# A fused attention and feed-forward kernel: the state of batch 0 is loaded by the ScalarE DMA queue instead of the SyncE queue

## Chip, cores and metric

The kernel runs on one core of one Trainium2 chip. The metric is the device time of one execution in microseconds (us), as the median of several runs.

## What is computed

For each of 8 batches and 8 heads there is a block `x` of 512 rows and a `state` of 32 rows, both 64 wide. Each attends to the other, and the joined rows (544 for each batch, 8 heads x 64 = 512 wide) go through a gated feed-forward layer with 1536 hidden columns. Inputs and output are float32.

```python
B, H, S, Ns, D = (8, 8, 512, 32, 64)
def _attn_ref(x, state):
    scores = scale * np.matmul(x, state.transpose(0, 1, 3, 2))
    a = softmax(scores)                      # over the 32 state rows
    xread = np.matmul(a, state)
    scores2 = scale * np.matmul(state, x.transpose(0, 1, 3, 2))
    a2 = softmax(scores2)                    # over the 512 rows of x
    sread = np.matmul(a2, x)
    return np.concatenate([xread, sread], axis=2)
def _moe_ref(x, w_gate, w_val, w_out):       # x: (8 * 544, 512)
    gate = np.maximum(x @ w_gate, 0.0)
    val = x @ w_val
    return gate * val @ w_out
```

(The softmax is written out in the reference; `scale` is 1/sqrt(64).)

## The kernel before

The attention output is never formed for the x rows. For each batch the kernel multiplies the state with the gate and value weights first (`u_mm`, L331, tile `u_ps`, evicted to `U`), and then the softmax weights, transposed (`ANS`), with `U` (`gv_mm`, L369, tile `gv_ps`). ScalarE takes the relu of the gate half (`gv_relu`, L381), VectorE multiplies it with the value half (`gv_mult`, L385), and `out_piece` (L407, tile `o_ps`) multiplies the result with the output weights. The rows of the state itself, 32 for each batch, come at the end for all batches together (`gvs`, L393).

The order of the instructions on each engine is written out by hand: the program is under a manual schedule (L462), so each engine runs its instructions in the order of the program text. First come L470 to L482: a memset for dummy matmuls, the identity matrix, a memset of `sz_b` on GpSimd (POOL), `st_dma(0, 1)` at L473 (the load of the state of batch 0), four loads of x of batch 0, two heads each (L474, L475, `x_dma` at L153), an activation on ScalarE (ACT) of a single column at L476, and VectorE (DVE) work for the permutation matrix (`make_perm`, L173) and columns of ones. Then the list `FIRST` (L17 to L65) is run through, a hand-made order of steps for batches 0 to 2; a loop over batches 2 to 7 (L527) does the rest. A step is a name and its arguments, with "a", "v" or "p" for ACT, DVE or POOL:

```python
FIRST = [
    ("dummy", 9), ("w", 0, 256, ("s", 0)), ("st_cast", 0, 1, "v"), ("st_mm", 0, 1), ("st", 1, 2),
    ("xl", 1, 0, 2, ("x", 0, 4)), ("xl", 1, 2, 2), ("xl", 1, 4, 2), ("xl", 1, 6, 2), ("st", 2, 3), ("dummy", 3),
    ("st_ev", 0, 1, "a"), ("conv", 0, 0, 2, "v"), ("xt", 0, 0), ("dummy", 1), ("conv", 0, 2, 2, "v"),
```

The names that matter here:

- `dummy` (L466): matmuls on zeros that keep TensorE (PE) busy.
- `st` (`st_dma`, L140): a load of state, 64 KB for one of the batches 0 to 2 (128 partitions of 512 bytes). `st_cast` (L181) turns it to bfloat16 (`st_b`), `st_mm` (L184) transposes it with four matmuls into `stT_ps`, and `st_ev` (L193) evicts that to `stT`.
- `xl` (`x_dma`): a load of x. A load of two heads has 256 KB, two runs of 1 KB in each partition. `conv` (L229) turns two heads to bfloat16 in `xs`, `xt` (L243) transposes them with four matmuls into `xT_ps`, `xe` (L248) evicts that to `xT`.
- `sc` (L254), `exp` (L270), `sum` (L275), `mul` (L280): scores, exponential on ACT, sum and reciprocal on DVE, product into `a_sn` on DVE or POOL. `at` and `ae` transpose `a_sn`.
- `w` (`w_dma`, L160): two loads of weights, gate and value, 256 columns each in the first steps (256 KB each), issued by POOL. `u` and `ue` are the matmuls of the state with these weights and their eviction, `g`, `gr`, `gm` the three steps of `gv`.

All loads of x and state, the DMA transposes and the stores are issued by the SyncE queue (SP), in the order of the program. `gate` (L135) makes a load wait for the landing of another: the first weight loads wait for the state of batch 0, `("s", 0)`; the loads of x of batch 1 wait for the third x load of batch 0, `("x", 0, 4)`; the second weight loads wait for the first gate weights.

Of the kernel before, what the change touches and what calls it, by code (L numbers as in the profile page):

```python
# [67 lines left out]
def kernel(  # L68
# [9 lines left out]
    nc = tc.nc  # L78
# [34 lines left out]
    st_f = const.tile([128, 3, 2, D], FP32, name="st_f")  # L113
# [21 lines left out]
    def gate(d, after):  # L135
        if after is not None:
            info = mybir.DependencyInfo(mybir.DependencyClass.Sync, mybir.DependencyReason.DATA)
            tc.add_manual_dep(d.ins, loads[after], info, reason="order of loads")

    def st_dma(lo, hi, after=None):  # L140
        if lo < 3:
            d = nc.sync.dma_start(out=st_f[:, lo:hi].rearrange("p b t d -> p b (t d)"),
                                  in_=state.rearrange("b h (m t) d -> (h m) b (t d)", t=2)[:, lo:hi])
        else:
            d = nc.sync.dma_start(out=sz_f.rearrange("p b g d -> p (b g) d"),
                                  in_=state[3:B].rearrange("b (g h) n d -> (h n) (b g) d", g=2))
        loads["s", lo] = d.ins.name
        gate(d, after)
# [322 lines left out]
    make_identity(nc, id128)  # L471
    nc.gpsimd.memset(sz_b, 0.0)
    st_dma(0, 1)  # L473
    for j in range(NJ):  # L474
        x_dma(0, 2 * j, 2)  # L475
# [5 lines left out]
    for i in range(3):  # L481
        set_ones(i)  # L482

    steps = {
        "dummy": dummies, "w": w_dma, "wo": wo_dma, "st": st_dma,
        "st_cast": st_cast, "st_mm": st_mm, "st_ev": st_ev, "st_z": st_z, "st_bar": st_bar, "conv": x_conv, "xc": x_copy, "xt": x_tr, "xe": x_ev,
        "sc": sc_mm, "exp": sc_exp, "sum": nrm_sum, "mul": nrm_mul, "at": a_tr, "ae": a_ev,
# [96 lines left out]
```

The softmax here doesn't subtract the row's maximum and nothing guards it: scores larger than these inputs give would overflow.

## Time and profile before

| | us |
|---|---|
| median of 8 runs | 225.65 |
| lowest and highest run | 224.53, 226.43 |
| the profiled execution, its time | 226.43 |
| the profiled execution, its span | 224.6 |
| busy in the span: PE, DVE, ACT, POOL | 216.7, 140.4, 114.3, 42.1 |
| `st_f` loads, issue to landing: shortest, longest | 1.8, 5.4 |
| `xf` loads of the first 6 us, issue to landing: shortest, longest | 2.9, 5.1 |

The span runs from the first instruction to the last. PE, DVE, ACT, POOL and SP are TensorE, VectorE, ScalarE, GpSimd and SyncE; PEld is TensorE's weight load; a q behind the name (SPq) is the engine's instruction queue, which issues DMAs. L156 is line 156 of the kernel; L128 and L126 are the helper `cp` on DVE and ACT. In a time line a row gives start and length in us, engine, line, operation, output<-input, shapes and the number of instructions, and in brackets how long the engine had been idle and what released it. The chain of waits goes back from the last instruction and names at each step what that step waited for.

### The profile page before, as it was taken

What the parts mean: (1) busy time and instruction counts of PE and PEld (TensorE: products, weight loads), DVE (VectorE), ACT (ScalarE), POOL (GpSimd) and SP (SyncE); (2) the same over time, 40 slices, a digit from 0 to 9 for tenths busy, and PEclk for the clock granted to TensorE, in tenths of its full rate; (3) what the DMA queues carried; (4) which work ended last, traced back from release to release, by engine and by line L of the source; (5) the groups of instructions that cost most, each with busy time, mean ns of one, the idle gap of its engine ahead of it and who ended that gap; (6) DMA issues with size and microseconds to landing.
All of it is one profiled execution on the core that took longest, in us unless ns stands there. A gap on an engine that the chain in (4) does not pass through costs nothing.

```text
span 224.6 us, 4848 instructions
## 1 busy us (share of the span) xinstructions
PE 216.7 (96%) x1931; PEld 107.2 (48%) x1953; DVE 140.4 (63%) x245; ACT 114.3 (51%) x212; POOL 42.1 (19%) x51
## 2 busy tenths in 40 slices
PE   7979999999999999999999999999999999999994
PEld 4654433344444444444444444444444444586543
DVE  5597889795577657866595659564956544442210
ACT  3656777576273647363745455455636344343112
POOL 6398004137070160007000700000000000000000
PEclk9997999999999999999999999999999999999999
DMA  5999998986954861295119811361131111110123
GB/s 179 247 223 188 218 247 156 214 204 157 234 160 103 234 139 50 56 271 129 53 39 268 143 47 47 96 146 50 47 93 57 47 47 50 47 47 28 69 74 113
DMA packets 43575, 28.17 MB, mean 125 GB/s; under 512 B 23840, under 2 KB 39328, under 8 KB 43552
## 3 DMA queue, kind: packets, MB, share of 16 engines
q1 hardware_dynamic: 36688, 23.14, 39.4%
q0 software_dynamic: 6864, 4.72, 14.3%
q8 instruction: 15, 0.25, 0.4%
q14 instruction: 8, 0.07, 0.1%
HBM read 18.35 MB, written 8.91 MB: 121 GB/s over the span
## 4 chain that ended last, share of the span: by engine, by line
PE 92%; DVE 2%; DMA 2%; issue 1%; SPq 1%; ACT 0%
PE o_ps L414 38%; PE gv_ps L377 38%; PE u_ps L325 6%; PE gvs_ps L399 5%; DMA xf<-in_x_dram 2%; PE sc_ps L260 2%; PE o_ps L439 1%; PE sr_ps L306 1%; DVE a_sn L283 1%; PE warm_ps L468 1%; SPq L156 1%; PE aT_ps L288 1%; DVE xs L128 0%; PE xT_ps L246 0%; DVE cs L277 0%
## 5 line engine op out<-in xcount | busy, mean ns | idle before, releaser
L386 DVE TENSOR_TENSOR h_sb<-gv_ps,g_sb 128x512 bf16<-128x512 f32 x96 | 65.7, 688 | 51.4 <-ACT g_sb L383 51.0
L377 PE MATMUL gv_ps<-ans,U 128*128 128x512 bf16 x384 | 95.3, 382 | 0.1
L414 PE MATMUL o_ps<-wo_sb,h_sb 128*128 128x512 bf16 x350 | 91.1, 379 | 1.4 <-issue 0.5
L383 ACT ACTIVATE g_sb<-gv_ps 128x512 bf16<-128x512 f32 x96 | 57.3, 597 | 54.7 <-PE gv_ps L377 53.9
L377 PEld LDWEIGHTS <-U 128*128 128x128 bf16 x384 | 36.2, 98 | 42.4 <-issue 1.8
L414 PEld LDWEIGHTS <-h_sb 128*128 128x128 bf16 x372 | 35.2, 98 | 43.4 <-issue 4.0
L126 ACT CAST U<-u_ps 128x512 bf16<-128x512 f32 x52 | 27.6, 595 | 7.1 <-PE u_ps L325 6.5
L128 DVE CAST U<-u_ps 128x512 bf16<-128x512 f32 x44 | 27.7, 674 | 1.7 <-PE u_ps L325 1.7
L130 POOL CAST xb<-xf 128x1024 bf16<-128x1024 f32 x11 | 11.2, 1041 | 72.0 <-DMA xf<-in_x_dram 72.0
L126 ACT COPY o_sb<-o_ps 128x512 f32<-128x512 f32 (+2 forms) x20 | 10.8, 540 | 18.7 <-PE o_ps L414 17.1
L128 DVE COPY o_sb<-o_ps 128x512 f32<-128x512 f32 (+2 forms) x18 | 11.4, 635 | 9.1 <-ACT o_sb L126 4.5
L271 ACT ACTIVATE e_sn<-sc_ps 128x512 bf16<-128x512 f32 (+1 forms) x18 | 9.8, 551 | 10.2 <-PE sc_ps L260 10.2
L403 DVE TENSOR_TENSOR hs_sb<-gvs_ps,g_sb 128x256 bf16<-128x256 f32 x12 | 5.1, 424 | 9.9 <-ACT g_sb L402 9.9
L130 POOL COPY xs<-xb 128x1024 bf16<-128x1024 bf16 x11 | 11.2, 1042 | 0.3
L277 DVE TENSOR_REDUCE cs<-e_sn 128x32 f32<-128x1024 bf16 (+2 forms) x13 | 10.4, 797 | 1.0 <-ACT e_sn L271 1.0
L325 PEld LDWEIGHTS <-stT 64*32 64x32 bf16 x560 | 6.0, 90 | 8.7 <-issue 7.0
L325 PE MATMUL u_ps<-wg_sb,stT 64*32 64x256 bf16 (+1 forms) x280 | 10.0, 318 | 0.0
L402 ACT ACTIVATE g_sb<-gvs_ps 128x256 bf16<-128x256 f32 x12 | 4.6, 384 | 10.2 <-PE gvs_ps L399 7.8
L325 PE MATMUL u_ps<-wv_sb,stT 64*32 64x256 bf16 (+1 forms) x280 | 9.6, 310 | 0.0
L468 PE MATMUL warm_ps<-warm 128*128 128x256 bf16 x37 | 8.4, 362 | 1.1 <-DVE warm L470 1.1
L283 DVE TENSOR_TENSOR a_sn<-e_sn,rc 128x1024 bf16<-128x1024 bf16 (+1 forms) x7 | 9.0, 1285 | 0.0
L260 PEld LDWEIGHTS <-xT 128*128 128x128 bf16 x128 | 6.6, 104 | 3.6 <-DMA xT<-xb 0.7
(52 smaller groups left out, 110.1 us busy)
## 6 DMA issues: line engine op xcount, KB each, us to landing
out_dram<-o_sb SPq DMA_DIRECT2D x31, 256.0 KB, 2.4
xf<-in_x_dram SPq DMA_DIRECT2D x6, 1024.0 KB, 6.9
xf<-in_x_dram SPq DMA_DIRECT2D x8, 256.0 KB, 5.1
wo_sb<-in_moe_w_out_dram POOLq DMA_DIRECT2D x3, 512.0 KB, 15.3
wg_sb<-in_moe_w_gate_dram POOLq DMA_DIRECT2D x4, 256.0 KB, 6.3
wv_sb<-in_moe_w_val_dram POOLq DMA_DIRECT2D x4, 256.0 KB, 6.7
wg_sb<-in_moe_w_gate_dram POOLq DMA_DIRECT2D x1, 512.0 KB, 9.4
wv_sb<-in_moe_w_val_dram POOLq DMA_DIRECT2D x1, 512.0 KB, 11.7
```

Source lines behind the costliest of these rows:

```text
L126: nc.scalar.copy(out=o, in_=i)
L128: nc.vector.tensor_copy(out=o, in_=i)
L130: nc.gpsimd.tensor_copy(out=o, in_=i)
L260: nc.tensor.matmul(ps_sc[b, kc][:, c, :, j2], xT[b][:, c, j], stT[:, b, j].rearrange("p (s n) -> p s n", s=2), start=True, stop=True)
L283: en.tensor_tensor(out=a, in0=e, in1=r.to_broadcast(list(e.shape)), op=ALU.mult)
L325: nc.tensor.matmul(ps[32 * j:32 * j + 32, 0:n], stT[r, b, j, 32 * kc:32 * kc + 32], wsb[w][r, j, lo:lo + n], start=(i == 0), stop=True, sk ...
L377: nc.tensor.matmul(ps.rearrange("p (c t) -> p c t", c=NC), U[b][:, kc, w, f0:f0 + 128], ANS[b][:, :, kc], start=(kc == 0), stop=(kc == 1))
L383: nc.scalar.activation(out=g_sbs[b, jf], in_=ps_g[b, jf][0], func=AF.Relu)
L386: nc.vector.tensor_tensor(out=hsb[b][:, jf], in0=ps_g[b, jf][1], in1=g_sbs[b, jf], op=ALU.mult)
L399: nc.tensor.matmul(ps[:, w].rearrange("p (b n) -> p b n", b=B), wsb[w][:, j, f0:f0 + 128], brT[:, :, 32 * j:32 * j + 32], start=(j == 0), ...
L414: nc.tensor.matmul(o_ps[0], src[:, jf, t0:t0 + 128], wo_sb[:, jf], start=(jf == 0), stop=(jf == NF - 1))
L468: nc.tensor.matmul(wps[:, 0:cols], warm[:, 0:128], warm[:, 0:cols], start=True, stop=True)
```

## The change

`st_dma` issues the load of the state of batch 0 (`lo == 0`, called at L473) on the ScalarE queue. The other loads of state stay on the SyncE queue. Source, destination, place in the program text and the waits on the load stay as they are.

```diff
     def st_dma(lo, hi, after=None):
         if lo < 3:
-            d = nc.sync.dma_start(out=st_f[:, lo:hi].rearrange("p b t d -> p b (t d)"),
-                                  in_=state.rearrange("b h (m t) d -> (h m) b (t d)", t=2)[:, lo:hi])
+            en = nc.scalar if lo == 0 else nc.sync
+            d = en.dma_start(out=st_f[:, lo:hi].rearrange("p b t d -> p b (t d)"),
+                             in_=state.rearrange("b h (m t) d -> (h m) b (t d)", t=2)[:, lo:hi])
         else:
```

## The prediction

> **What bounds the kernel now.** I read the engine table first, then the windows table, then the chain of waits for the first 22 us, then the time lines of SP, ACT, DVE, PE and POOL there, and the DMA rate. The page says that the kernel as a whole is a TensorE kernel:
>
> ```profile
> PE 216.7 (96%) x1931; PEld 107.2 (48%) x1953; DVE 140.4 (63%) x245; ACT 114.3 (51%) x212; POOL 42.1 (19%) x51
> PEclk9997999999999999999999999999999999999999
> ```
>
> The idle time of PE is 224.6 − 216.7 = 7.9 us, and the windows table puts 3.38 us of it ahead of 17.9 us, where the steady matmuls begin (columns: window, its length, busy us of PE, PEld, DVE, ACT and POOL with the number of instructions, granted clock, DMA share, GB/s):
>
> ```profile
> 0.00:17.90 17.90, 14.52 (x182) 9.77 (x183) 12.24 (x33) 9.55 (x20) 12.17 (x21) 0.96 1.08 212
> 17.90:224.60 206.70, 202.15 (x1751) 97.41 (x1770) 128.19 (x213) 104.80 (x192) 29.95 (x30) 1.00 0.50 118
> ```
>
> After 17.9 us the chain is PE behind PE, so a start that comes earlier by d should end earlier by about d. What sets the start is seen in the chain of its first 22 us (start, length, what):
>
> ```profile
> 0.74 0.40 SPq L142
> 1.14 0.06 issue
> 1.20 0.41 SPq L156
> ...
> 2.68 5.13 DMA xf<-in_x_dram
> 7.81 0.02 issue
> 7.83 0.44 DVE xs L128
> 8.27 0.05 issue
> 8.32 0.61 PE xT_ps L246 x4
> ...
> 12.43 2.35 DVE a_sn L283
> ```
>
> The very first step of the chain is SP's issue of the state, 0.40 us, and behind it the four issues of x of batch 0; the fourth lands at 7.81 us. The engines that the change touches, at that time:
>
> ```profile
> 0.73 1.28 ACT L476 ACT_TABLE_LOAD   x1 [0.73 <-PEq L568]
> 3.77 0.37 ACT L126 CAST stT<-stT_ps 128x256 bf16<-128x256 f32 x1 [1.53 <-PE stT_ps L189]
> 2.67 0.34 DVE L128 CAST st_b<-st_f 128x128 bf16<-128x128 f32 x1
> 4.81 0.61 PE L246 MATMUL xT_ps<-id,xs 128*128 128x128 bf16 x4 [0.34 <-DVE xs L128]
> 2.82 0.94 POOL L162 DMA_DIRECT2D wg_sb<-in_moe_w_gate_dram  x1 [0.40 <-DMA st_f<-in_state_dram]
> ```
>
> PE waits 0.34 us for the first conversion of x and later 0.33 us for the fourth: 0.67 us in all that earlier x could remove. POOL's first weight load waits for the landing of the state.
>
> **What the Trainium skill says.** "DMA: Bandwidth & Descriptors", section "Issuing engines are not separate DMA queues": DMAs issued by several engines run on the same 16 DMA engines; issuing from two saves only the sequencer's issue time. Here that is 0.46 us (1.20 − 0.74), and the trace shows it on the chain; no row of before has a load issued by ACT. Same page, section "Queues, rings and completion order": each DMA engine takes turns between queues, packet by packet. The trace agrees in kind: the fourth x load, beside POOL's weight load, takes 5.13 us to land against 2.9 us for the first. "Perfetto Trace Analysis", section "DMA Instruction — HWDGE (DVE, Sync)": the descriptor generator is locked by one issuer at a time; no run here shows two issuers. "TensorE: Matmul & The Clock Gate", Part 1, section "What's actually happening": the clock is judged in free-running windows of 3413 ns; the 7 in the PEclk line is such a stretch, at 16.8 to 22.4 us, and I take it as scatter.
>
> **The change, part by part.**
>
> 1. *SP loses one issue.* The four x loads of batch 0 and the second state load behind them start 1.20 − 0.74 = 0.46 us earlier. Is the path free for them? The DMA rate in steps of 0.1 us shows the state's packets from about 1.7 to 2.2 us and x from 2.3 us, that is 1.1 us after its issue (1.20), much as the state came 1.0 us after its own. So x was not queued behind the state, and its first packets move by nearly the whole 0.46 us. From then on the bytes are what counts: the state's 64 KB now share the engines with x, and at the 256 to 389 GB/s of 3.0 to 4.0 us they cost 0.16 to 0.26 us. Earlier landing of each x load: 0.46 − 0.2 = 0.26 us; 0.46 if the state slips in for nothing; 0 if the generator's lock lets SP's first load begin only after ACT's 0.40 us. I take 0.3.
>
> 2. *The fourth x load meets less.* It lands late since weight packets share the engines with it. Earlier by 0.3 us, and the weights perhaps later (step 4), it should run more alone: earlier by 0.5 us or more (bounds 0 and 1.2, the latter if it lands 3.9 us after its issue of 2.22). But only 0.33 us of PE wait is there to be won, as PE comes free at 8.32 − 0.33 = 7.99 us.
>
> 3. *ACT gains one issue*, ahead of the activation of L476: 0.40 to 0.47 us by SP's three rows of the same load. Table load and first activation then end at about 2.7 instead of 2.23 us. The next work of ACT is at 3.77 us, after 1.53 us of idling: 1.1 us of cover, so nothing; without cover it would cost the 0.46. No wait is added on ACT: the load goes into a fresh tile.
>
> 4. *The state lands later.* Now it lands 1.8 us after issue, at 2.55 us. Queued behind it: the cast on DVE (2.67 us), four matmuls (3.08), three dummies (to 4.47), the first transposes (4.81); on POOL the first weight loads. In the change it runs beside x: 512 B for each partition against 2 × 1 KB, taken in turns, so some 64 + 128 KB pass before it is complete. At the 154 to 276 GB/s of the first x packets that is 0.7 to 1.2 us against the 0.5 us now: later by 0.2 to 0.7. At best it is through first: 0. I take 0.3. Of this the cast hides about 0.1 (DVE is at memsets till 2.96). On PE the 0.34 us wait of the first transposes covers it: x converts at about 4.45 instead of 4.76, but PE comes free at 4.47 + 0.25 = 4.7, so the first transposes win 0.1 us, not 0.34. They would win all 0.34 if the state came no later.
>
> 5. *From there to 10 us.* The steps between the first and fourth transposes wait on each other (PE, ACT, PE), not on DMA. So at the fourth transposes: 0.1 from step 4 plus 0.33 from step 2, 0.43 us; with bounds of 0 and 0.67.
>
> 6. *Weights.* The first pair is issued 0.3 us later; by the rows of 0 to 8 us it lands 6.2 and 6.7 us after issue, so at 9.0 and 10.45 us, and its first reader is the matmul at 11.41 us: 0.96 us of cover for 0.3 late plus 0.43 early. Covered. The second pair waits for the first's landing but is issued only at 9.56, held by the POOL product before it: cover 0.5 us, just enough. So POOL too moves up by 0.2 to 0.8 us; I take the same 0.4 to 0.5.
>
> 7. *DVE at 12.43.* The product of 128x256 takes 2.35 us on the chain, 0.50 us at 9.39. In the long one POOL runs conversion, product, conversion from 12.73 to 14.49, and DVE is through 0.3 us after. If both engines move by the same, it stays so. If DVE moves up 0.1 to 0.3 us more than POOL, it is through before POOL begins, and PE's wait of 1.37 us at 15.18 us goes (rival B).
>
> Sum: −0.43 us by PE waits; some 0.1 more, as the conversions of the fourth load, sums and products on DVE come up to 0.5 us sooner and the chain runs over them till 12.4 us: −0.55. The profiled execution took 226.43 us, 1.83 more than its span of 224.6; the sum against it gives 225.88. That execution is the slowest of the eight shown, so the same step against their median of 225.65 gives 225.1.
>
> **Rivals.** 0.3% (0.68 us) is about what a measurement of this kernel can tell from no change; faster is below 224.97, slower above 226.33.
>
> A, forecast, 44%: a shift of 0.3 to 1.0 us, 224.65 to 225.35, likeliest 225.1; 20 of the 44 lie beyond 0.68.
> B, the product on DVE slips ahead of POOL, 18%: 0.43 + 1.37 = 1.8 us at most, some 1.2 to 1.8, so 223.85 to 224.45. For it: it misses by about 0.1 us now. Against: both engines hang on the same loads and may move together.
> C, the transfer is hidden anyway, 18%: the generator is locked in turn, or the state's lateness eats all of PE's wait; 225.4 to 225.9. For it: PE is 96% busy. Against: DVE idles 1.14, 0.96 and 1.17 us for x.
> D, slower, 20%: the state starves at the DMA engines or is issued after ACT's 1.28 us table load. It decides from about 0.45 us of lateness (0.1 + 0.34 of cover): beyond that every tenth shifts cast, transposes and weights. With the table load first, lateness is 1.28 + 0.3 = 1.6, less the cover 0.45, 1.1 us: 226.8; with starving by 1.2 us, 226.4. For it: x loads with four times the bytes are now ahead of the state. Against: the table load is booked to L476, which stands after the load.
>
> The change can't fail to happen: SP must lose the row.
>
> **How the numbers follow.** Faster 18 + 20 = 38, same 24 + 18 = 42, slower 20. The range leaves out a tenth at each side: half of B's part below 224.2, and half of D's above 226.4.
>
> **What would show it.** Step 1: SP's first row is x at 0.74 us, and DVE's first conversion of x begins at 3.7 to 3.9 us. Step 3: an ACT DMA row at 0.73, the table load after it. Step 4: DVE's cast at 2.9 to 3.1 us, POOL's weight load 0.3 us later. Steps 2 and 5: the fourth conversion before 7.4 us, its transposes at about 7.9. Step 7: the DVE product still above 2 us. Wrong: a cast after 3.4 us (D), a product of 0.5 us at 12 us (B), or steady matmuls that start no earlier than 17.7 us (C).

## The result and the profile after

The changed kernel takes 226.69 us (median of 19 runs, 225.22 to 227.98) against 225.38 us for the kernel before in the same measurement (56 runs): ratio 1.0057 with a 95% interval of 1.0038 to 1.0076. It is slower by 1.3 us. (A ratio leaves out executions in the slow state and medians keep them, so a ratio below can differ from the quotient of two medians by up to 0.3%.) The forecast of 225.1 us was wrong in sign, and the time lies above the range of 224.2 to 226.4 us.

The two profiled executions hide most of this: 226.92 us and a span of 225.1 us after, 226.43 and 224.6 before, 0.5 us apart. The kernel before was caught with its clock dip; from its first to its seventeenth matmul of `gv`, L377, it needs 6.95 us where the changed kernel needs 5.98. A second profile of the kernel before, without a dip, has a span of 222.5 us; the dip is about half of that difference, the rest is told under step 7 below.

The engine table and clock row of the changed kernel (columns as before):

```profile
PE 215.2 (96%) x1931; PEld 106.1 (47%) x1953; DVE 140.9 (63%) x245; ACT 114.3 (51%) x212; POOL 41.7 (19%) x51
PEclk9999999999999999999999999999999999999999
```

The windows table, cut at the same place:

```profile
0.00:17.90 17.90, 13.51 (x177) 8.60 (x177) 11.97 (x32) 9.53 (x20) 11.29 (x21) 1.00 1.10 197
17.90:225.10 207.20, 201.72 (x1754) 97.52 (x1776) 128.91 (x213) 104.75 (x193) 30.41 (x31) 1.00 0.50 119
```

The clock is whole, so PE needs fewer busy us; but ahead of 17.9 us it idles 4.39 us instead of 3.38, and after it 5.48 us instead of 4.55. Both stretches lost about 1 us. The time lines of the start show the steps that the prediction spoke of (start, length, engine, line, operation; in brackets the idle time and what ended it):

```profile
0.74 0.42 ACTq L143 DMA_DIRECT2D st_f<-in_state_dram  x1
1.19 1.28 ACT L477 ACT_TABLE_LOAD   x1 [1.19 <-PEq L569]
4.15 0.37 ACT L126 CAST stT<-stT_ps 128x256 bf16<-128x256 f32 x1 [1.46 <-PE stT_ps L190]
...
3.18 0.23 DVE L128 CAST st_b<-st_f 128x128 bf16<-128x128 f32 x1 [0.23 <-DMA st_f<-in_state_dram]
...
7.62 0.39 PE L247 MATMUL xT_ps<-id,xs 128*128 128x128 bf16 x4
11.90 0.30 PE L326 MATMUL u_ps<-wv_sb,stT 64*32 64x256 bf16 x8 [1.03 <-DMA wv_sb<-in_moe_w_val_dram]
...
3.46 0.94 POOL L163 DMA_DIRECT2D wg_sb<-in_moe_w_gate_dram  x1 [1.04 <-DMA st_f<-in_state_dram]
10.72 0.80 POOL L163 DMA_DIRECT2D wg_sb<-in_moe_w_gate_dram  x1 [2.28 <-DMA wg_sb<-in_moe_w_gate_dram]
```

The fourth transposes of batch 0 come at 7.62 us instead of 8.32. Then the gain is lost: the value weights keep PE waiting 1.03 us, and POOL's second pair of weight loads goes out at 10.72 instead of 9.56 us. In the kernel before PE reads the value weights without a wait (a row has no bracket when the engine was idle for less than 0.15 us):

```profile
11.53 0.29 PE L325 MATMUL u_ps<-wv_sb,stT 64*32 64x256 bf16 x8
```

The chain of waits has a new member, the loads of x of batch 1:

```profile
0.74 0.46 SPq L157
...
1.76 4.04 DMA xf<-in_x_dram
...
5.81 0.37 SPq L157
...
6.79 7.24 DMA xf<-in_x_dram
...
14.05 1.75 DVE xs L128
```

The second loss lies far from the change. The chain around 124 us, in the loop:

```profile
122.09 1.21 DVE U L128 x2
123.29 0.51 SPq L318
...
123.92 6.18 DMA xT<-xb
...
130.14 0.41 PE sc_ps L261 x8
```

In PE's time line that step is a wait of 0.83 us, which the kernel before hasn't got (the changed kernel first):

```profile
130.14 0.41 PE L261 MATMUL sc_ps<-stT,xT 128*128 128x64 bf16 x8 [0.83 <-DMA xT<-xb]
```

```profile
129.66 0.41 PE L260 MATMUL sc_ps<-stT,xT 128*128 128x64 bf16 x8
```

The DMA table for 116 to 122 us tells what else is there (q14 is a queue of the kind "instruction": number of packets, MB, share of the 16 engines; then loads and transposes with the us from issue to landing of the last part). The changed kernel, and after it the kernel before:

```profile
q14 instruction: 1, 0.01, 0.3%
...
xf<-in_x_dram SPq DMA_DIRECT2D x1, 1024.0 KB, 7.8
...
ans<-a_sn SPq DMA_TRANSPOSE x1, 3.8
```

```profile
xf<-in_x_dram SPq DMA_DIRECT2D x1, 1024.0 KB, 6.9
...
ans<-a_sn SPq DMA_TRANSPOSE x1, 3.1
```

Every DMA reports its landing in 16 parts. In the changed kernel 15 parts of these `ans` transposes are in by 3.12 us and the last at 3.84; of the x load by 6.68 and 7.79; of the `xT` transposes behind them by 5.44 and 6.18. Before, `ans` and x end without such a straggler (3.07 and 3.09, 6.69 and 6.86); `xT` has one there too (4.97 and 5.65), but PE doesn't wait for it. What has moved is a packet of 8192 bytes. The kernel before has two of them here, 6.7 and 7.3 us after the issue of `ans`; the changed kernel has one after 2.5 us (309 ns long), just ahead of the landing, and one after 7.8 us.

### The profile page after: what moved, and what is told of

Same layout as the page of the kernel before. It is cut to its first block, busy times and chain, and to the rows that moved or that the text cites. A ratio compares the mean times of both kernels' runs of the same rounds, so it can differ in the third digit from the quotient of the medians.

```text
span 225.1 us, 4848 instructions
## 1 busy us (share of the span) xinstructions
PE 215.2 (96%) x1931; PEld 106.1 (47%) x1953; DVE 140.9 (63%) x245; ACT 114.3 (51%) x212; POOL 41.7 (19%) x51
## 4 chain that ended last, share of the span: by engine, by line
PE 84%; DMA 10%; DVE 2%; SPq 1%; issue 1%; ACT 0%
PE o_ps L415 35%; PE gv_ps L378 35%; DMA xT<-xb 5%; PE u_ps L326 5%; DMA xf<-in_x_dram 5%; PE gvs_ps L400 5%; PE sc_ps L261 2%; PE o_ps L440 1%; PE sr_ps L307 1%; DVE U L128 1%; SPq L157 1%; DVE xs L128 1%; PE aT_ps L289 1%; SPq L318 0%; DVE ans L128 0%
## 5 line engine op out<-in xcount | busy, mean ns | idle before, releaser
L469 PE MATMUL warm_ps<-warm 128*128 128x256 bf16 x37 | 7.7, 337 | 1.1 <-DVE warm L471 1.1
L261 PEld LDWEIGHTS <-xT 128*128 128x128 bf16 x128 | 6.0, 100 | 5.0 <-DMA xT<-xb 1.9
L261 PE MATMUL sc_ps<-stT,xT 128*128 128x64 bf16 x128 | 7.3, 196 | 1.0 <-DMA xT<-xb 0.8
```

The lines of the kernel that those rows point to most:

```text
L261: nc.tensor.matmul(ps_sc[b, kc][:, c, :, j2], xT[b][:, c, j], stT[:, b, j].rearrange("p (s n) -> p s n", s=2), start=True, stop=True)
```

## The experiments

All times are medians; the ratio is against the kernel before in the same measurement, with its 95% interval. "Fetch" is the start in us of the first 8 KB packet of that queue near the `ans` transposes of about 116 us, counted from their issue; "wait" is PE's idle time for `xT` at about 130 us in the profiled execution, and 0 stands for 0.1 us or less.

| kernel | edit | us | ratio | fetch | wait |
|---|---|---|---|---|---|
| the change | | 226.69 | 1.0057 [1.0038, 1.0076] | +2.5 | 0.83 |
| e0 | before, unchanged | 225.27 | 1.0005 [0.9985, 1.0025] | +6.7 | 0 |
| e1 | before, weights issued late | 225.36 | 1.0023 [1.0003, 1.0043] | +6.6 | 0 |
| e2 | change, weights not gated | 227.17 | 1.0092 [1.0058, 1.0126] | +2.5 | 0.93 |
| e3 | change, small load ahead of x | 226.93 | 1.0108 [1.0068, 1.0148] | +2.4 | 1.09 |
| e4 | change, x of batch 1 later | 226.47 | 1.0070 [1.0048, 1.0093] | +2.5 | 1.40 |
| e5 | before, weights not gated | 226.96 | 1.0086 [1.0059, 1.0113] | +6.8 | 0 |
| e6 | before, +1 on ScalarE | 227.14 | 1.0063 [1.0043, 1.0082] | +2.5 | 1.38 |
| e7 | change, -1 on ScalarE | 226.12 | 1.0022 [0.9996, 1.0048] | +7.1 | 0.16 |
| e8 | before, +6 | 225.12 | 0.9995 [0.9975, 1.0015] | -1.7 | 0 |
| e9 | change, +5 | 226.37 | 1.0050 [1.0026, 1.0074] | -1.7 | 0.18 |
| e10 | change, -1, weights not gated | 226.04 | 1.0014 [0.9991, 1.0036] | +6.7 | 0 |
| e11 | before, -1 | 225.07 | 1.0009 [0.9990, 1.0028] | +6.7 | 0 |
| f1 | the change again | 227.14 | 1.0091 [1.0067, 1.0115] | +2.5 | 1.21 |
| f2 | e9 again | 226.03 | 1.0035 [1.0016, 1.0055] | -1.7 | 0.14 |
| f3 | e7 again | 225.60 | 1.0027 [1.0001, 1.0052] | +6.8 | 0 |
| f4 | change, +5, weights not gated | 225.10 | 1.0005 [0.9982, 1.0029] | -1.4 | 0 |

### First theory: the late weights (e1, e2, e3)

The first suspicion was that the first weight loads, held by the state until 3.46 instead of 2.82 us, are what costs. e1 keeps them late in the kernel before, behind one more memset on POOL; e2 takes the state's gate away in the changed kernel; e3 gives the changed kernel's x loads their old start.

```diff
 # e1, on the kernel before, after L472
+    nc.gpsimd.memset(sz_b[:, 0:4], 0.0)
 # e2, on the changed kernel
-    ("dummy", 9), ("w", 0, 256, ("s", 0)), ("st_cast", 0, 1, "v"), ...
+    ("dummy", 9), ("w", 0, 256), ("st_cast", 0, 1, "v"), ...
 # e3, on the changed kernel, ahead of the loads of x
+    pad = const.tile([128, D], FP32, name="pad")
+    nc.sync.dma_start(out=pad[0:1], in_=state[0, 0, 0:1])
```

> The kernel before, with one more memset of four fifths of sz_b on GpSimd ahead of the first weight loads: these are issued at about 3.4 us instead of 2.82, as in the changed kernel, while every load of state and x stays as before. Theory W (the changed kernel is slower since the late state makes the first weights late): slower than before by 0.8 to 1.5 us, the value weights landing at 11 us or later. Rival X (the loads of x that come earlier press on the weights; their own late issue matters little): within 0.4 us of before. Rival Q (something of the ScalarE queue itself): same as before.

Measured: 225.36 us, ratio 1.0023. The weights went out at 3.39 us, and yet the first gate weights landed at 9.09 us, which is also the mean of five kernels with the old start, and the value weights at 10.47 us, not at 11 or later. A late issue alone doesn't land late; the theory in this simple form fell.

> The changed kernel, with the first weight loads no longer gated on the landing of the state: issued at about 2.5 us instead of 3.46. Theory W: the loss goes, and the gain at the fourth transposes (0.7 us in the trace of after) is kept: 0 to 0.8 us faster than before. Rival X: still slower than before by 0.8 us or more, as the loads of x stay early. Rival Q: still slower by 1.3 us.

Measured: 227.17 us, not better than the change. The start did get better: the 65th matmul of `gv` begins at 35.1 us, against 35.8 to 36.6 us in three profiles with the changed start and no dip (the change, e9, f1). But PE now waits 1.92 us for `xT` at 45.6 us and 0.93 us at 130.6.

> The changed kernel, with a load of a single row of 256 bytes ahead of the x loads on SP, so that x is issued at about 1.2 us as before while the state stays on ScalarE. It tells the queue from the time of x. Theory W: the state lands at 2.6 us, the first weights are issued at 2.8, the time is that of before within 0.4 us. Rival X: the same, as x is at its old time. Rival Q: slower by about 1.3 us, as the changed kernel.

Measured: 226.93 us. The fourth x load landed at 8.9 us, later than in either kernel, so the edit overshot and says little. But the wait at 130 us was there again, 1.09 us, in three kernels with three different starts. That pointed away from the start.

### What stands in the loop is the ScalarE program (e0, e4, e5, e6, e7)

e4 and e5 still varied the start; e0 is the kernel before as a mark. e6 and e7 test the new theory: the change gives ScalarE one more instruction, and this moves the fetch of instructions. e6 adds a second tiny activation to the kernel before, e7 removes the tiny activation of the changed kernel (its result is not used), so that the number is again that of before.

```diff
 # e4, on the changed kernel
-    ("xl", 1, 0, 2, ("x", 0, 4)), ("xl", 1, 2, 2), ...
+    ("xl", 1, 0, 2, ("x", 0, 6)), ("xl", 1, 2, 2), ...
 # e5, on the kernel before
-    ("dummy", 9), ("w", 0, 256, ("s", 0)), ...
+    ("dummy", 9), ("w", 0, 256), ...
 # e6, on the kernel before, after L476; e7 removes this line from the changed kernel
+    nc.scalar.activation(out=tiny, in_=nc.const_aps.tensor(0.0, (128, 1), FP32), func=AF.Exp)
```

> The kernel before once more, unchanged, for a second trace: the profiled execution on record lost about 1 us to a stretch of half clock at 16.7 to 20.1 us, which 25 of 28 other executions did not have. Every theory expects the time of before, and a trace whose steady matmuls begin before 17.9 us and whose 64th of them comes about 1 us earlier than 37.55 us.

> The changed kernel, with the x loads of batch 1 gated on the fourth x load of batch 0 instead of the third: issued at about 6.6 us instead of 5.81. Theory X2 (the first weights land late since the x loads of batch 1 run into their tail): the first gate weights land at 10.0 us or earlier instead of 10.68, and it is 0.3 to 0.8 us faster than the changed kernel, so within 0.5 to 1.0 us of before. Rival W (their late issue alone): they land at 10.7 us still, and the time is that of the changed kernel, 1.3 us slower than before.

> The kernel before, with the first weight loads not gated on the state: issued at about 2.45 us instead of 2.82. Theory W: the weights land up to 0.4 us earlier; they had 0.9 us of cover, so little: 0 to 0.4 us faster. Rival X: as before within 0.3 us. If earlier weights press on the fourth load of x instead, it is slower by up to 0.4 us.

Measured: 225.27, 226.47 and 226.96 us. Holding x of batch 1 back (e4) lets the gate weights land at 9.99 us, as expected, but the time isn't better: the third load of x still lands at 13.70 us (12.73 in the mean of five kernels with the old start), and PE waits twice for `xT`, 2.03 us at 46.3 and 1.40 at 131.7. e5 shows the other side of the gate: with the weights issued at 2.36 us the fourth x load lands at 8.82 instead of 7.81 us, and PE waits for its conversion. It was slower by more than the 0.4 us expected; five of its six executions had a stretch of half clock, and PE waits 0.84 us for `ans` at 58.7 us and 0.50 us for `xT` at 61.1 us besides, so the size of this effect isn't known.

```profile
9.33 0.61 PE L246 MATMUL xT_ps<-id,xs 128*128 128x128 bf16 x4 [0.83 <-DVE xs L128]
```

> The kernel before, with the one-column activation of L476 done twice: one more instruction (0.2 us) in an idle stretch of ScalarE. All three kernels with the state on ScalarE lose 1.0 us at 130 us, where the transposed load of x waits; in all of them the DMA queue of kind instruction has a piece at 118 to 120 us that the others have at 122 to 125 us. Theory F (one more instruction on ScalarE moves the fetch of its instructions onto the transfers of that time): this kernel loses it too, 0.7 to 1.2 us slower than before, the x load of 118 us landing 7.5 us or more after its issue instead of 6.9. Rival (the loss hangs on the second queue itself): as before within 0.3 us.

> The changed kernel without the one-column activation of L476, which computes nothing that is used: as many instructions on ScalarE as before. Theory F: the x load of 118 us lands 6.9 us after its issue and the wait at 130 us goes; 0.7 to 1.2 us faster than the changed kernel, 0.2 to 0.6 us slower than before. Rival (the queue itself): the wait at 130 us stays, time as the changed kernel, 1.3 us slower than before.

Measured: e6 227.14 us, ratio 1.0063, the size of the change's own loss, with state and x issued as before. In its profile PE's wait at 130 us and the fetch are there (PE's time line, then the DMA table of 116 to 119 us):

```profile
129.42 0.41 PE L260 MATMUL sc_ps<-stT,xT 128*128 128x64 bf16 x8 [1.38 <-DMA xT<-xb]
```

```profile
q14 instruction: 1, 0.01, 0.6%
...
xf<-in_x_dram SPq DMA_DIRECT2D x1, 1024.0 KB, 8.4
```

e7: 226.12 us, ratio 1.0022; the wait is down to 0.16 us. So one activation of 0.20 us, which ScalarE does while it has nothing else to do, decides over more than half of the loss, by the ratio (1.0022 against 1.0057, with intervals that overlap).

### Number or place (e8 to e11)

Does each further ScalarE instruction cost, or does it matter where the fetch falls? e8 replaces the tiny activation in the kernel before by seven, e9 that of the changed kernel by six. e10 and e11 have one fewer.

```diff
 # e8, on the kernel before (e9: range(6), on the changed kernel)
-    nc.scalar.activation(out=tiny, ...)
+    for _ in range(7):
+        nc.scalar.activation(out=tiny, ...)
 # e10 removes the activation from the changed kernel, and the gate of the first weights as e2 does
 # e11 removes the activation from the kernel before
```

> The kernel before with seven tiny activations in a row at the start of ScalarE in place of one; they end about 2.5 us later, while ScalarE has no work. One instruction more cost 1.3 us (ratio 1.0063), with a fetch of the queue named instruction at 2.4 us after the ans transposes of 116 us instead of 6.7 us after. Theory of place (what decides is where that fetch falls): six instructions move it away, or by another interval; if it no longer falls between 116 and 119 us there is no wait above 0.3 us at 130 us, and the time is within 0.3% of before, 224.8 to 225.9 us. Rival, theory of count (any added instruction of ScalarE costs about 1.3 us, wherever the fetch falls): 226.3 us or more, ratio 1.005 or more.

Measured: 225.12 us, ratio 0.9995. Six more instructions cost nothing; one more cost 1.4 us. The fetch is now at 113.7 us, ahead of the transfers, and in the stretch of 116 to 122 us no packet of q14 is left; x and `ans` land on time, and PE's row has no bracket:

```profile
xf<-in_x_dram SPq DMA_DIRECT2D x1, 1024.0 KB, 6.6
...
ans<-a_sn SPq DMA_TRANSPOSE x1, 3.1
```

```profile
128.86 0.40 PE L260 MATMUL sc_ps<-stT,xT 128*128 128x64 bf16 x8
```

> The changed kernel with six tiny activations in place of one. Theory of place: as with six more in the kernel before, the fetch of the queue named instruction leaves the stretch of 116 to 119 us, the wait at 130 us falls from 0.83 us to under 0.3 us, and the time is 225.0 to 226.0 us, 1 us under the changed kernel's. Theory of count: 226.5 us or more, no better than the changed kernel.

Measured: 226.37 us, ratio 1.0050. The wait at 130 us is 0.18 us as the theory of place has it, but the time isn't back. This expectation missed: the changed kernel must lose something else as well.

> The changed kernel without its tiny activation (so with as many ScalarE instructions as before, which gave ratio 1.0022) and with the first weight load no longer waiting for the state. Theory that the late weights are what the start still loses: the first pair lands about 0.9 us earlier, the 1.03 us wait for the value weights falls under 0.3 us, and the time is 224.3 to 225.2 us, a little under before. Rival, that what TensorE gains before 42 us is taken back at the transposes of 46 us, or that the earlier weights press on the fourth x load as they did in the kernel before (ratio 1.0086): 225.2 to 227 us, no gain or a loss.

> The kernel before without its tiny activation, so with one ScalarE instruction less than before. Theory of place: the fetch at 123 us moves, or stays; if it stays off the stretch of 116 to 119 us nothing changes, 224.7 to 225.7 us, ratio 0.997 to 1.003; with the fetch on another x load, a wait at that load's transposes and 0.5 to 1.3 us lost. Theory of count: one instruction less gains some of what one more cost, 224.0 to 224.6 us.

Measured: e10 226.04 us, ratio 1.0014; e11 225.07 us, ratio 1.0009. Neither differs from the kernel before; e10 had been expected a little ahead of it.

The profiles measure the loop by itself. From the 209th to the 301st matmul of `gv` the six kernels with the fetch at +2.4 to +2.5 us take 46.8 to 47.3 us, the twelve others, with the kernel f4 below among them, 45.8 to 46.1. So e9's loop is cured (46.1 us), and its loss lies ahead of the loop: its 209th matmul begins at 111.9 us (111.5 in f1, 112.4 in the change), in three profiles with the old start and no dip (e0, e6, e11) at 110.5 to 111.1 us.

### How the loss divides (f1 to f4)

f1 is the change again, f2 is e9 and f3 is e7 once more; f4 is e9 with the gate of the first weights taken away (the diff of e2), so that both suspected parts are undone.

> The changed kernel once more, as the mark for the three kernels beside it. Both theories: 226.2 to 227.0 us, ratio 1.0045 to 1.009. Two parts theory: about half of it lies ahead of the loop (weights and second x batch land late) and half in the wait at 130 us. One part theory: it is nearly all the wait at 130 us.

> The changed kernel with six tiny activations, which took the wait at 130 us away in its profile and yet gave ratio 1.0050. Two parts theory: the start's loss stays, ratio 1.002 to 1.005, 225.6 to 226.3 us. One part theory: the earlier result was a chance of few runs, ratio 0.998 to 1.002.

> The changed kernel without the tiny activation, which took the wait away in the other direction and gave ratio 1.0022. Two parts theory: the same time as with six tiny activations, ratio 1.002 to 1.005. One part theory: 0.998 to 1.002.

> The changed kernel with six tiny activations and the first weight load no longer behind the state: both suspected parts undone. Two parts theory: ratio 0.998 to 1.002, about 0.8 us under the kernel that has the six activations alone. One part theory: no different from that kernel. A third outcome, the earlier weights press on the fourth x load as in the kernel before with the same edit: 1.004 or more.

Measured: 227.14, 226.03, 225.60 and 225.10 us against 225.04. There are two parts. With the fetch out of the way four measurements give 1.0022, 1.0027, 1.0035 and 1.0050, in the mean 1.0034 or 0.75 us: the start's part. With the weights released as well there is no loss that can be told from none (f4 1.0005, e10 1.0014; the intervals reach 1.0029 and 1.0036, so some of the 0.75 us may be left). PE's rows of the value weights, in f2 and in f4, show it:

```profile
11.65 0.30 PE L326 MATMUL u_ps<-wv_sb,stT 64*32 64x256 bf16 x8 [1.00 <-DMA wv_sb<-in_moe_w_val_dram]
```

```profile
11.16 0.29 PE L326 MATMUL u_ps<-wv_sb,stT 64*32 64x256 bf16 x8
```

Five more idle ScalarE instructions are the only difference between e2 and f4: 227.17 and 225.10 us. But not all of this is the fetch at 116 us. In the profiles e2 loses 1.1 us against f4 in the loop (46.9 and 45.8 us for the stretch above), and 2.0 us between the 65th and 129th matmul of `gv`, where its wait at 45.6 us lies. So e2, whose start was no worse than f4's, could tell neither for nor against the late weights.

## Why the prediction was wrong

**Step 1 held.** SP's first row is x at 0.74 us; the first three x loads land 0.18, 0.23 and 0.42 us earlier, around the 0.3 us taken. SP's and ACT's first issues run side by side (0.74 to 1.20 and 0.74 to 1.16 us), so the bound in which SP waits for ACT's 0.40 us did not come true.

**Steps 2 and 5 held in direction, and were too small.** The fourth x load lands at 6.53 instead of 7.81 us, and its transposes come 0.70 us earlier against the 0.43 forecast. The landing 1.28 us earlier lies outside the bound of 1.2 us, which was a slip: a landing 3.9 us after an issue at 2.22 us would be 1.7 us earlier. It landed 4.27 us after its issue.

**Step 3 failed, and with it most of the sum.** It put the price of ScalarE's extra issue at nothing: "1.1 us of cover, so nothing". For the engine's own work this is right: the eviction of `stT` comes after 1.46 us of idling. But an instruction is also a place in the program that is fetched. e6 put one more instruction on ScalarE without moving any transfer and lost 1.4 us. Of all 18 profiles the six with exactly one more ScalarE instruction than the kernel before (the change, e2, e3, e4, e6, f1) have the fetch 2.4 to 2.5 us after `ans`, one of the 16 parts of `ans` 0.7 us late, the x load at 7.8 to 8.4 us instead of 6.2 to 7.0, and a wait of 0.8 to 1.4 us at 130 us. The twelve others have the fetch elsewhere and a wait of at most 0.18 us. So the premise that after 17.9 us the chain is PE behind PE fell too: in the changed kernel it runs over `xT` at 124 us. In the six, the first 15 parts of `xT` are in 3.94 to 3.99 us after the last part of that x load (4.0 to 5.2 us in the others), which suggests that the late part of x is what `xT` and PE wait for.

The same mark stands at other places too. Of 377 DMA transposes in the 18 profiles, 35 have their last part more than 0.5 us behind the fifteenth, and in all 35 an instruction packet starts 0.2 to 1.0 us before that fifteenth part. With a packet of 8 KB (14 cases, each 309 ns long) the last part is 0.66 to 0.78 us late, with one of 16 KB (21 cases, 0.89 to 1.42 us long) 1.47 to 1.91 us. Of 329 transposes without such a packet in the 1.1 us before, none is later than 0.47 us; but 13 with one aren't late either. The waits of e2 and e4 at 45.6 and 46.3 us carry the mark: a 16 KB packet starts 0.46 and 0.48 us ahead, and the last part of `xT` is 1.57 and 1.55 us late. A late part costs nothing where nothing waits for it: the kernel before has one of 1.51 us in the `ans` transposes of 139.5 us.

The change also takes an instruction from SyncE, and this leaves a mark of its own. In all ten profiles with 153 instructions on SP, it stands still for 0.44 to 0.46 us ahead of the `brT` transposes near 122 us, in the eight with 154 for 0.06 us; `xT` goes out 8.2 us after `ans` instead of 7.8, and a second 8 KB packet comes 7.7 to 7.9 us after it instead of 6.7 to 6.8. This uses up cover, but it doesn't make the wait: e6 has the wait without it, f4 and e10 have it without the wait. It was seen in the profiles alone; no run separates it.

The Trainium skill bears on this in "Runtime: NRT & Kernel Launch", section "Instruction fetch mechanics": the sequencer fetches ahead over a DMA queue of its own, in blocks of 16 KiB, and the cost is mostly hidden. The profile shows such a queue of 16 KB pieces (q8), and one of 8 KB pieces (q14), half the block that the page names. That the engine doesn't wait agrees: ScalarE's relu at 118.18 us comes after the usual 1.13 us of idling. What isn't hidden is the fetch's price for the data beside it.

**Step 4 was mis-sized.** The state lands 2.42 us after its issue instead of 1.79; the cast comes 0.51 us later and the weight load 0.64, against 0.3, inside the bounds given. The first transposes came 0.14 us earlier all the same, near the 0.1 forecast.

**Step 6 failed.** It took the landing at 6.2 and 6.7 us after the issue and called the first pair covered. In the changed kernel this was 6.98 and 7.48 us. (The cover was even 1.1 us: the value weights are first read at 11.53 us, not at 11.41.) And the prediction followed the transfers of batch 0 only; it left out the loads of x of batch 1, which share the DMA engines with the weights. Landing of the last part, mean and range over kernels with the same start:

| us | fourth x of batch 0 | gate weights | value weights | third x of batch 1 |
|---|---|---|---|---|
| start as before (before, e0, e6, e8, e11) | 7.53 | 9.09 (8.73 to 9.42) | 10.49 | 12.73 (12.38 to 13.06) |
| changed (after, e7, e9, f1, f2, f3) | 6.64 | 10.00 (9.64 to 10.44) | 11.38 | 13.60 (13.26 to 14.03) |
| changed, weights not gated (e2, e10, f4) | 7.73 | 8.94 (8.36 to 9.26) | 10.36 | 12.56 (12.00 to 12.86) |

What the fourth x load gains, 0.9 us, the weights and x of batch 1 lose, 0.9 us each; released weights turn both back. It is the same traffic in another order, and of the two the later transfers are on the chain. Which of the two moves, x earlier or weights later, makes the weights land so late isn't separated: late alone (e1) doesn't.

**Step 7 was right that this spot moves the time, but not that it hangs on the change.** In the changed kernel the product is short, as in rival B, yet the DVE conversion behind it is now the long one (1.75 us at 14.05 us, beside POOL's three steps), and PE still waits 1.03 us:

```profile
13.18 0.40 DVE L284 TENSOR_TENSOR a_sn<-e_sn,rc 128x256 bf16<-128x256 bf16 x1
```

The kernel before itself does either. In its second profile (e0) product and conversion take 0.82 and 0.84 us, and the wait of 1.37 us is gone:

```profile
11.89 0.82 DVE L283 TENSOR_TENSOR a_sn<-e_sn,rc 128x256 bf16<-128x256 bf16 x1
12.63 0.84 DVE L128 CAST xs<-xf 128x512 bf16<-128x512 f32 x1
```

Its steady matmuls begin at 15.7 us; in e6 and e11, with the same start of the loads but the long conversion, at 16.8 and 17.0. So the start of one profile is uncertain by about 1 us, and how often each kernel's executions fall to either side isn't known; a part of the start's 0.75 us could lie here.

**Of the rivals D had the sign.** Its mechanism (a state starved or behind the table load) isn't what happened: the table load stayed behind the issue, at 1.19 us, and the state was 0.6 us late. Only its point that weights shift with the state beyond 0.45 us of lateness lies near the start's part.

**What stays open.** The start's 0.75 us and e6's 1.4 us add to more than the 1.3 us of the first measurement, and near the 2.0 us of f1; the two parts are not known to better than about 0.5 us. That the ScalarE program decides over the loss in the loop is shown by e6 and e8, and agrees with e7 and e9. That it works through the 8 KB packet rests on its place in 18 profiles and on the late parts; the packet couldn't be moved by itself. No record names the engine that a packet belongs to. If the one that stays with SyncE's program is SyncE's, ScalarE's moved from 7.3 to 2.5 us by one instruction more, and to 1.7 us ahead of `ans` by six; why so far is not explained.

No version beat the kernel before: f4, e8, e10 and e11 equal it.

## What to carry to other kernels

Where a kernel's transfers are timed to within a microsecond, an instruction added to an idle engine isn't always free, even with full cover: compare where the packets of the queues named "instruction" fall before and after, and whether one of 16 parts of a transfer is late. To test such a suspicion, add and remove a few useless instructions on that engine; if one more costs and six more don't, it is a matter of place, not of work. And when a load moves to another queue, list all transfers of the next 15 us, not only those that wait for it: what one gains in shared DMA engines another loses.

## What the runs showed of the hardware

- Where an instruction packet starts within the 1.1 us before the fifteenth of a DMA transpose's 16 parts lands, the last part is often late: in 35 of 48 cases, by 0.66 to 0.78 us with 8 KB and by 1.47 to 1.91 us with 16 KB. The delay is beyond the packet's own 0.31 and 0.89 to 1.42 us. In the six kernels with the loss one part of the 1 MB load behind `ans` came 1.1 to 2.3 us after the fifteenth.
- A load of 64 KB issued on ScalarE's queue while SP's x loads run landed after 2.42 us, on SP's queue ahead of them after 1.79.
- The DVE conversion of 128x512 took 0.43 us while POOL was idle, and 1.70 to 1.83 us in nine profiles where POOL worked during 1.57 to 1.70 us of it.
- A run with a stretch of half clock early on, as in the first profile of the kernel before, costs about 1 us in that stretch (6.95 against 5.98 us for the same 16 matmuls), as much as the effect sought here; a single profile of each kernel, compared by its span, would have told little.
